# Dense FFN of a fused kernel: fewer plain units, longer segments, sums added into the output by transfers

## The chip, the cores and the metric

One core of a Trainium2 chip runs the whole program. The metric is the device time of one execution in microseconds, measured several times; the profile is one further execution, recorded by the hardware profiler. The engines are PE (matmul), PEld (its weight load), DVE (VectorE), ACT (ScalarE), POOL (GpSimd) and SP (SyncE, which here only issues transfers).

## The reference, cut to what matters

```python
# 1 windowed attention: 4 batches x 8 heads, 576 positions, head size 64, window 64
# 2 soft mixture of experts on x (2304 x 512): 32 slots, 8 experts, w1 512x1024, w2 1024x512
    d = softmax(x @ phi over tokens);  slot_input = d.T @ x
    slot_out[e] = np.maximum(slot_input[e] @ w1[e], 0.0) @ w2[e]
    x = softmax(x @ phi over slots) @ slot_out            # c @ slot_out
# 3 dense FFN on x (2304 tokens x 512), w_in 512x2048, w_out 2048x512, both float64
    h = x @ w_in
    g = np.maximum(h, 0.0) + np.log1p(np.exp(-np.abs(h)))   # softplus
    return (g @ w_out).astype(np.float32)
```

## The kernel before, in words

Parts 1 and 2 of the reference fill the first 124 us. There PE, DVE, ACT and the loads share the work, and the change doesn't touch them until the last product of the experts' second layer (`emit_l2`, L865). What follows is called stage 2 here.

In stage 2 the 2304 tokens are 18 tiles of 128, in five groups of 4, 4, 4, 4 and 2 (`GROUPS`), and the 2048 hidden columns are 16 units of 128. Since the input of the FFN is `c @ slot_out` with 32 slots, `h` is made from `c` (kept transposed as `cT`) and from `slot_out @ w_in` (`wst`, made by the steps WD, WA, WQ, WL, WB, PC, PS from the slots' outputs `soT` and the converted `w_in`), so one matmul gives the 128 hidden columns of a unit for a whole group of tokens.

Both FFN weights come as float64 in `raw` (16 + 16 pieces of 512 KB) and are made float32 on the chip by four operations of 512 columns each (`conv`, step C): a scaling (ACT L970 or DVE L972), and three of integers on DVE (L976, L977, L978).

The first `NN` = 8 units are plain units. For each item (a unit for a group of tiles): H, a matmul 128x512 (L1144); G, softplus on ACT (L1148); GH, its rounding `gh` on ACT (L1009); GL, the rest `gl` = g - gh on DVE (L1012); and for each tile Y, three matmuls 128x512 (L1168 to L1170: gh x high, gh x low, gl x high part of w_out) that add in a PSUM bank. The units of a group go in slabs (`SLABS`, up to two per group). At the end of a group's first slab the bank is copied to `part` in SBUF by ACT (step O, L1009), and at the end of its second slab DVE adds the bank to `part` (L1178).

The other 8 units go in `NP` = 4 pairs, by block products: for two units and a group of tiles, seven products of sums of blocks replace eight. DVE and ACT form the sums on the side of the weights (TA, TB, TC, TK, TM, TH, TL into `thi`, `tlo`) and of the tokens (G2, XA, XB, XC, HG, LG, HX, LX into `shl`); P is one product, for each pair of tiles three matmuls 128x256 (L1249). After a group's four pairs ACT copies each of seven banks (MC, L1257) and DVE adds it into two or one blocks of `part` (M, L1267 and L1273); SP then stores the group's tiles (L1278, 256 KB each).

Every engine runs its own instructions in the order in which they are written. That order comes from `plan()`, which lists the steps with what each needs, and `arrange()`, which goes through them in order of due time with random shifts (`TWEAKS`). Nothing of it is decided on the chip: an engine whose next instruction lacks an input waits, and all behind it wait.

Of the kernel before, what the change touches and what calls it, by code (L numbers as in the profile page):

```python
# [25 lines left out]
NN = 8  # L26
SLABS = ((0, 1, NN), (0, 2, NN), (0, 3, NN), (0, 4, NN), (0, 4, NN))
# [5 lines left out]
NG, NH = 3, 4  # L33
# [3 lines left out]
NCT = 1  # L37
# [10 lines left out]
L2_END, GOAL, SLACK, NEAR = 6.4, 12.0, 0.65, 0.1  # L48
# [16 lines left out]
def arrange(steps, free, ports, tweaks=(), modes=None, slack=SLACK, near=NEAR):  # L65
# [21 lines left out]
    for k in steps:  # L87
        latest[k] += shift[k]
# [65 lines left out]
def plan():  # L154
# [13 lines left out]

    for h in range(2):
        step(("SO", h), dict(D=0.35), rel=L2_END + 0.42 * h - 0.3)  # L170
        step(("ST", h), dict(E=0.43), [("SO", h)])
        step(("SE", h), dict(A=0.26, D=0.33), [("ST", h)])
    for n, r in enumerate(RAWS):
# [16 lines left out]
        elif kind == "wo":  # L190
            if u == 1:
                deps = [("C", "wo", j, x, 3) for x in range(2)] + [(k, j - 1) for k in ("TH", "TL")]
                deps += used_up(max(j - 4, -1)) if 2 * (j - 4) >= NN else []
# [3 lines left out]
                room = [("Y", i, y) for i, x in enumerate(ITEMS) for y in range(x[4], x[5]) if x[1] in (2 * (2 * j - NN - 4), 2 * (2 * j - NN - 4) + 1, 2 * (2 * j - NN - 3), 2 * (2 * j - NN - 3) + 1)] if 2 * j - NN >= 4 else []  # L197
# [22 lines left out]
    for b in range(NCT, 4):  # L220
        step(("CT", b), dict(E=0.48), [("CE", b - 3), ("WD", 0, 1)])
        step(("CE", b), dict(A=0.52, D=0.61), [("CT", b)])
# [9 lines left out]
    for i, (g, f, first, last, ta, tb) in enumerate(ITEMS):  # L232
        n = 128 * (tb - ta)
        b = HBANK[i]
        step(("H", i), dict(E=n * 0.000456), [unit(f)] + weights(START[g] + ta, tb - ta) + ([held[b]] if b in held else []))
# [4 lines left out]
        if i >= NDIRECT:  # L240
            step(("GH", i), dict(A=0.1 + n * 0.00083, D=0.075 + n / 1920), [("G", i)] + [("Y", i - NH, j) for j in range(4)])
        step(("GL", i), dict(P=n * 0.00238, D=0.075 + n / 960), [("GH", i), ("G", i)])
        for j in range(ta, tb):
            deps = [("GH", i), ("GL", i), ("SH", f), ("SL", f), ("Y", i, j - 1)]
            if first:
                deps += [("O", x, j) for x in range(max(0, i - 24), i)] + [("PS", 0)] * (j == 2) + [("CE", x) for x in ((2,), (1,), (), (3,))[j]]
            else:
                deps += [("Y", x, j) for x in range(max(0, i - 2), i) if ITEMS[x][0] == g]
            step(("Y", i, j), dict(E=0.7), deps, goal=goal)
            goal += 0.7  # L250
            if last:
                step(("O", i, j), dict(A=0.49, D=0.61) if f < SLABS[g][1] else dict(D=0.61), [("Y", i, j)])
# [7 lines left out]
    for s, (g, p) in enumerate(PAIRS):  # L260
# [7 lines left out]
        xs = [(k, s - 1 - (s > 1)) for k in ("HX", "LX")] + [("C",) + RAWS[-1] + (3,)] + [(k, NN // 2 + NP - 1) for k in ("TH", "TL") if s > 1]  # L268
# [7 lines left out]
        for i, (b, x, y) in enumerate(PRODUCTS):  # L276
# [42 lines left out]
def block_kernel(ctx: ExitStack, tc: tile.TileContext, qk, v, phi, w1, w2, w_in, w_out, out):  # L319
# [468 lines left out]
    with tc.manual_schedule():  # L788
# [132 lines left out]
        for b in (*range(NCT), 4):  # L921
            do_ct("E", b)
# [428 lines left out]
```

## Time and profile before

| | before |
|---|---|
| median of 3 runs | 351.93 us (351.89 to 352.76) |
| the profiled execution's own time | 351.86 us |
| its span, first to last instruction | 350.2 us |
| granted TensorE clock, mean | 0.998 |
| PE busy | 338.5 us, 97% |
| DVE busy | 286.6 us, 82% |
| ACT busy | 205.7 us, 59% |
| POOL busy | 65.2 us, 19% (all of it before 130 us) |
| read from and written to memory | 64.63 and 4.72 MB |

The span is the time between the first and the last instruction in the trace, and 1.66 us of the profiled execution lie outside it. Busy shares are means over stages that differ; the places that matter here are read from the stages. Start-to-start distance of two instructions of one kind that follow each other without a wait is what one of them costs its engine's queue; the duration of a single instruction is a little longer, since the next one begins before it ends.

### The profile page before, as it was taken

The page shows a single profiled execution, that of the slowest core. Times are in us where ns is not written, and L with a number is a line of the kernel's source. Part 1 is how long each engine was busy: PE and PEld are TensorE (multiplying, and loading weights), DVE is VectorE, ACT ScalarE, POOL GpSimd, SP SyncE. Part 2 cuts the span into 40 slices and gives each one's busy share as a digit, 9 for nine tenths or more (in the row PEclk, how much of TensorE's full clock was granted, in tenths as well). Part 3 has the DMA queues.
Part 4 walks back from the last instruction along what each step waited for, and adds up shares of the span by engine and source line. Part 5 has one row for each costly group of instructions (what it writes and reads, how often), then busy time and mean ns, then how long its engine had stood idle before and what let it go on. Part 6 is the DMA issues. An engine that isn't in the chain of part 4 may idle for free.

```text
span 350.2 us, 8448 instructions
## 1 busy us (share of the span) xinstructions
PE 338.5 (97%) x3298; PEld 273.4 (78%) x3298; DVE 286.6 (82%) x767; ACT 205.7 (59%) x385; POOL 65.2 (19%) x93
## 2 busy tenths in 40 slices
PE   8899998999999999999999999999999999999994
PEld 6788786877434366887788887788999999999994
DVE  5687776875452289999999996988988999999996
ACT  1676565756330069957976465455658568585660
POOL 4997766862040000000000000000000000000000
PEclk9999999999999999999999999999999999999999
DMA  7999999999999984547476300000000030210304
GB/s 283 410 411 403 411 407 409 407 416 393 405 409 417 414 327 161 185 193 242 137 255 210 120 0 3 1 0 2 0 2 0 2 120 2 83 41 0 122 2 181
DMA packets 18184, 69.89 MB, mean 200 GB/s; under 512 B 2016, under 2 KB 2400, under 8 KB 14304
## 3 DMA queue, kind: packets, MB, share of 16 engines
q1 hardware_dynamic: 18000, 69.09, 51.3%
q8 instruction: 26, 0.43, 0.5%
q10 hardware_dynamic: 144, 0.26, 0.2%
q14 instruction: 14, 0.11, 0.1%
HBM read 64.63 MB, written 4.72 MB: 198 GB/s over the span
## 4 chain that ended last, share of the span: by engine, by line
PE 87%; DVE 5%; issue 2%; DMA 1%; ACT 1%; POOL 1%; SPq 0%; DVEq 0%; POOLq 0%; ACTq 0%
PE m_ps L1249 21%; PE y_ps L1168 10%; PE y_ps L1169 10%; PE y_ps L1170 10%; PE x_ps L508 5%; PE pt_ps L490 5%; PE s_ps L463 4%; PE l_ps L815 4%; PE l_ps L865 4%; PE xt_ps L531 2%; PE h_ps L1144 2%; PE h_ps L1186 2%; DVE part L1267 1%; DMA v_three<-v_d 1%; PE lt_ps L541 1%
## 5 line engine op out<-in xcount | busy, mean ns | idle before, releaser
L1249 PE MATMUL m_ps<-thi,shl 128*128 128x256 f32 x504 | 87.7, 283 | 0.0
L1249 PEld LDWEIGHTS m_ps<-thi,shl 128*128 128x128 f32 x504 | 74.8, 190 | 1.4
L1168 PE MATMUL y_ps<-whl,gh 128*128 128x512 f32 x144 | 57.3, 398 | 0.0
L1169 PE MATMUL y_ps<-whl,gh 128*128 128x512 f32 x144 | 57.2, 397 | 0.0
L1170 PE MATMUL y_ps<-whl,gl 128*128 128x512 f32 x144 | 56.8, 395 | 0.0
L1249 PE MATMUL m_ps<-tlo,shl 128*128 128x256 f32 x252 | 53.0, 283 | 0.0
L474 DVE CUSTOM_DVE_ANT_0 sm<-s_ps,cst_sb 128x128 f32<-128x128 f32 x144 | 32.1, 287 | 12.0 <-PE s_ps L463 11.3
L1249 PEld LDWEIGHTS m_ps<-tlo,shl 128*128 128x128 f32 x252 | 40.0, 190 | 0.0
L481 POOL TENSOR_TENSOR sm<-mx,sm 128x512 f32<-128x512 f32 x36 | 36.6, 1039 | 7.2 <-DVE mx L474 6.3
L1168 PEld LDWEIGHTS y_ps<-whl,gh 128*128 128x128 f32 x144 | 27.0, 188 | 9.4 <-issue 1.7
L1148 ACT ACTIVATE g<-h_ps 128x512 f32<-128x512 f32 (+3 forms) x41 | 22.4, 552 | 19.8 <-PE h_ps L1144 19.3
L1206 ACT ACTIVATE g<-h_ps 128x512 f32<-128x512 f32 (+1 forms) x40 | 22.2, 556 | 19.5 <-PE h_ps L1186 19.3
L1170 PEld LDWEIGHTS y_ps<-whl,gl 128*128 128x128 f32 x144 | 27.0, 188 | 7.0 <-DVE gl L1012 0.6
L1169 PEld LDWEIGHTS y_ps<-whl,gh 128*128 128x128 f32 x144 | 27.1, 188 | 5.8
L484 ACT ACTIVATE sm<-sm 128x512 f32<-128x512 f32 x36 | 22.4, 634 | 11.6 <-POOL sm L481 11.4
L428 ACT COPY pt<-pt_ps 128x512 f32<-128x512 f32 x36 | 19.6, 588 | 11.9 <-PE pt_ps L490 11.6
L1009 ACT CAST gh<-g 128x512 fp32r<-128x512 f32 (+2 forms) x40 | 23.0, 581 | 4.6 <-PE y_ps L1169 4.1
L1012 DVE TENSOR_TENSOR gl<-g,gh 128x512 fp32r<-128x512 f32 (+3 forms) x41 | 25.2, 621 | 0.5 <-ACT gh L1009 0.3
L463 PE MATMUL s_ps<-qkb 64*64 64x128 f32 x576 | 20.7, 276 | 1.3 <-issue 1.2
L977 DVE SCALAR_TENSOR_TENSOR cvx<-raw,cvx 128x512 int32<-128x512 int32 x32 | 21.5, 686 | 0.1
L508 PE MATMUL x_ps<-vd,pt 128*64 128x65 f32 x288 | 21.1, 225 | 0.4 <-ACT sm L484 0.4
L508 PEld LDWEIGHTS x_ps<-vd,pt 128*64 128x64 f32 x288 | 18.4, 137 | 3.8 <-issue 2.2
(180 smaller groups left out, 648.2 us busy)
## 6 DMA issues: line engine op xcount, KB each, us to landing
w1t<-w_d SPq DMA_DIRECT2D x15, 1024.0 KB, 10.8
w2t<-w_d SPq DMA_DIRECT2D x13, 1024.0 KB, 10.3
qkb<-qk_d SPq DMA_DIRECT2D x17, 512.0 KB, 10.0
raw<-w_in_d SPq DMA_DIRECT2D x16, 512.0 KB, 4.8
raw<-w_out_d SPq DMA_DIRECT2D x16, 512.0 KB, 5.6
out_d<-part SPq DMA_DIRECT2D x17, 256.0 KB, 2.3
v_three<-v_d SPq DMA_DIRECT2D x10, 260.0 KB, 8.9
vt<-v_d SPq DMA_DIRECT2D x8, 260.0 KB, 9.1
```

Of the source, the lines that this page charges most:

```text
L463: nc.tensor.matmul(s_ps[2 * t + a][64 * par:64 * par + 64, 128 * p:128 * p + 128], qkb[rows, b, 0, p, 64 * par:64 * par + 64], rhs, start= ...
L474: nc.vector.tensor_tensor_reduce(out=sm[:, p], in0=ps[:, 128 * p:128 * p + 128], in1=mask, scale=-0.125, scalar=3.0e38, op0=ALU.add, op1=A ...
L481: nc.gpsimd.tensor_tensor(out=sm_t[i], in0=mb, in1=sm_t[i], op=ALU.subtract)
L484: nc.scalar.activation(out=sm_t[i], in_=sm_t[i], func=AF.Exp)
L508: nc.tensor.matmul(x_ps[64 * par:64 * par + 64, a, 65 * p:65 * p + 65], pt[:, 128 * p + 64 * par:128 * p + 64 * par + 64], vt[:, 65 * h:65 ...
L1009: (nc.scalar.copy if e == "A" else nc.vector.tensor_copy)(dst, src)
L1012: eng[e].tensor_tensor(out=dst, in0=a, in1=b.bitcast(F32), op=ALU.subtract)
L1148: nc.scalar.activation(out=st["g", i], in_=st["h", i], func=AF.Softplus)
L1168: nc.tensor.matmul(y, st["gh", i][:, ts], hi, start=first, stop=False)
L1169: nc.tensor.matmul(y, st["gh", i][:, ts], lo, start=False, stop=False)
L1170: nc.tensor.matmul(y, st["gl", i][:, ts], hi, start=False, stop=last)
L1249: nc.tensor.matmul(ps[:, 256 * j:256 * j + 256], s_tile(s, a)[:, w * x + 128 * j:w * x + 128 * j + 128], t, start=p == 0 and n == 0 and j ...
```

## The change

Units 6 and 7 become a fifth pair (`NN` 8 to 6, `NP` 4 to 5). The plain units no longer go by groups of four tiles but by segments of six tiles (`SEGS`), which hold six banks and leave bank 6 for H; items are three tiles wide (384 columns). Tiles 0 to 5 are done in two segments (units 0 and 1 first, 2 to 5 last), the other twelve in one.

Step O is now always a copy out of PSUM (ACT, or DVE): into a staging slot, from which a transfer issued by GpSimd writes the tile to the output, or, for the second time of tiles 0 to 5, adds it to the output in memory. Only tiles 16 and 17 stay in SBUF (`last_c`). At a group's end the sums of the seven products are made in a buffer of their own (`c_tile`): ACT writes the first two products of a group, each into two blocks (L1309); the others go by copy (L1312) and DVE addition (L1322, L1326) as before. For groups 0 to 3 a transfer of GpSimd adds each half of the group (512 KB) to the output (L1333); the last group is stored by SP as before.

The transition is also rewritten: the last w2 arrives as two halves, its product is 16 matmuls of 128 columns in one bank, split in two parts; the slots' outputs are summed by one DVE copy of 128 columns, one matmul and two copies; two pieces of `cT` are made after that product's first half instead of earlier. `shl` is two fixed sets of tiles. The order tables (`TWEAKS`, a new `SHIFTS`) are other ones; the core of the rest:

```diff
-NN = 8
-SLABS = ((0, 1, NN), (0, 2, NN), (0, 3, NN), (0, 4, NN), (0, 4, NN))
+NN = 6
+SEGS = ((0, 6, 0, 2), (6, 6, 0, NN), (12, 6, 0, NN), (0, 6, 2, NN))
+CUTS = ((0, 1, 3), (0, 3))
...
-HBANK = [4 + i % 3 for i in range(len(ITEMS))]
-PRODUCTS = ((2, 5, 3), (3, 6, 2), (4, 0, 6), (5, 1, 5), (6, 4, 4), (0, 3, 1), (1, 2, 0))
+HBANK = [6, 4, 5] + [6] * (len(ITEMS) - 3)
+PRODUCTS = ((6, 5, 3), (0, 6, 2), (1, 0, 6), (2, 1, 5), (3, 4, 4), (4, 3, 1), (5, 2, 0))
...
-            else:
-                l2_end.extend(bank(x, "l2_end") for x in (2, 7))
-                parts = [(y, 256 * h, 256, True, True) for h, y in enumerate(l2_end)]
...
+            for a in rows:
+                for kk in range(4):
+                    nc.tensor.matmul(
+                        l2_end[0][32 * kk:32 * kk + 32, 0:128], hTz[e // 2][:, e % 2, 4 * r + a, :], w_tiles["w2", j][a][:, 128 * kk:128 * kk + 128],
+                        start=a == 0, stop=a == 3,
                     )
...
+        emit_l2(N2 - 1, (0, 1))
+        do_ct("E", 4)
+        do_ce("A", 4)
...
+        emit_l2(N2 - 1, (2, 3))
+        do_ct("E", 0)
...
-        def do_so(e, h):
-            o = so[:, 256 * h:256 * h + 256]
-            nc.vector.tensor_tensor(out=o, in0=l2_end[h][:, 0:256], in1=o, op=ALU.add)
+        def do_so(e):
+            copy(e, so_end, l2_end[0][:, 0:128])
+
+        def do_st(e):
+            nc.tensor.matmul(so_ps[:, 0:128], so_end, ident, start=False, stop=True, skip_group_check=True)
...
         def do_o(e, i, j):
-            g, f = ITEMS[i][:2]
-            y = y_t.pop((g, j))
-            if f == SLABS[g][1] - 1:
-                copy(e, part[g, j], y)
+            t = TILE_OF[ITEMS[i][0]] + j
+            y = y_t.pop((ITEMS[i][0], j))
+            again = LAST_O[t][0] != (i, j)
+            if t < START[-1]:
+                x = stages[n_st[0] % len(stages)]
+                n_st[0] += 1
+                copy(e, x, y)
+                nc.gpsimd.dma_start(out=rows(t, 1), in_=x.rearrange("p (t c) -> p t c", t=1), **(dict(accum_op=ALU.add) if again else {}))
             else:
-                nc.vector.tensor_tensor(out=part[g, j], in0=y, in1=part[g, j], op=ALU.add)
+                x = last_c[:, 512 * (t - START[-1]):512 * (t - START[-1]) + 512]
...
+            if k in (5, 6):
+                o, m = both(c_tile(g), ps.rearrange("p (t c) -> p t c", t=nj), 0, int(k == 5), 512 * nj)
+                nc.scalar.mul(o, m, -1.0 if k == 5 else 1.0)
+                return
...
+                o = rows(START[g] + nj * a, nj)
+                if g == len(GROUPS) - 1:
+                    nc.sync.dma_start(out=o[:, :, c0:c1], in_=v[:, a, :, c0:c1])
+                else:
+                    nc.gpsimd.dma_start(out=o, in_=v[:, a], accum_op=ALU.add)
```

How the rows stand now, at three places. First DVE from the first conversion on, before (`L1026` adds the last w2's product, `L1012 wst` is a rest of the FFN's first weights):

```order
405 L972 TENSOR_SCALAR cvx<-raw 128x512
406 L976 TENSOR_SCALAR cvx<-cvx 128x512
407 L977 SCALAR_TENSOR_TENSOR cvx<-raw,cvx 128x512
408 L978 SCALAR_TENSOR_TENSOR wit<-raw,cvx 128x512
409 L1026 TENSOR_TENSOR wit<-l_end,wit 128x256 x2
410 L976 TENSOR_SCALAR cvx<-cvx 128x512
411 L972 TENSOR_SCALAR cvx<-raw 128x512
```

And the same place in the changed kernel:

```order
403 L988 TENSOR_SCALAR cvx<-raw 128x512
404 L992 TENSOR_SCALAR cvx<-cvx 128x512
405 L993 SCALAR_TENSOR_TENSOR cvx<-raw,cvx 128x512
406 L994 SCALAR_TENSOR_TENSOR wit<-raw,cvx 128x512
407 L1031 COPY cst_sb<-l_end 128x128
408 L988 TENSOR_SCALAR cvx<-raw 128x512
409 L1031 COPY part<-so_ps 128x256
410 L992 TENSOR_SCALAR cvx<-cvx 128x512
```

The two additions of 256 columns are gone; a copy of 128 columns and one of the two copies to `soT` stand on DVE in their place.

Second DVE late in the plain stage, before (`L1178` is the second O, `tlo` and `txs` sums of a pair's weights):

```order
546 L1178 TENSOR_TENSOR part<-y_ps,part 128x512
547 L1078 TENSOR_TENSOR txs<-wot 128x256
548 L1178 TENSOR_TENSOR part<-y_ps,part 128x512
549 L1012 TENSOR_TENSOR gl<-g,gh 128x512
550 L1178 TENSOR_TENSOR part<-y_ps,part 128x512
551 L1012 TENSOR_TENSOR gl<-g,gh 128x512
552 L1012 TENSOR_TENSOR tlo<-wot,thi 128x512
553 L1012 TENSOR_TENSOR tlo<-txs,thi 128x1280
```

And in the changed kernel, at the part of the plain stage with the second pair's weights:

```order
523 L993 SCALAR_TENSOR_TENSOR cvx<-raw,cvx 128x512
524 L994 SCALAR_TENSOR_TENSOR wot<-raw,cvx 128x512
525 L994 SCALAR_TENSOR_TENSOR wit<-raw,cvx 128x512 x2
526 L992 TENSOR_SCALAR cvx<-cvx 128x512
527 L1034 TENSOR_TENSOR t<-txs,t 128x1280
528 L1034 TENSOR_TENSOR gl<-g,gh 128x384
529 L993 SCALAR_TENSOR_TENSOR cvx<-raw,cvx 128x512
530 L1034 TENSOR_TENSOR gl<-g,gh 128x384
531 L994 SCALAR_TENSOR_TENSOR wot<-raw,cvx 128x512
```

The additions of O have left DVE; conversions stand between the `gl` of the plain units up to the end of that stage.

Third GpSimd's queue after the first stage, in the changed kernel:

```order
64 L920 TENSOR_TENSOR cc_1968<-lnat,cc_1968 128x2x32
65 L1213 DMA out_d<-part 128x512 x6
66 L1152 CAST identr<-cst_sb 128x128
67 L1213 DMA out_d<-part 128x512 x16
68 L1333 DMA out_d<-part 128x2x512 x8
69 L1402 UNCONDITIONAL_BRANCH
```

Before, that queue ended with the one cast; now 22 transfers of a tile and 8 of two tiles are issued there, and the cast stands behind the first six.

## Rows read from the trace of the kernel before

**Rows 1.** Windows: busy us of each engine, its instructions, PE clock, DMA share, GB/s.

```profile
130.00:140.00 10.00, 10.00 (x51) 7.21 (x51) 9.90 (x21) 9.77 (x23) 0.00 (x0) 1.00 0.52 177
140.00:150.00 10.00, 10.00 (x46) 8.13 (x45) 9.90 (x20) 9.92 (x20) 0.00 (x0) 1.00 0.64 215
...
130.70:203.60 72.90, 72.90 (x326) 56.93 (x325) 72.40 (x137) 55.18 (x105) 0.00 (x0) 1.00 0.53 183
...
210.00:220.00 10.00, 10.00 (x48) 7.16 (x47) 6.74 (x12) 5.25 (x8) 0.00 (x0) 1.00 0.01 2
...
260.00:270.00 10.00, 10.00 (x82) 9.82 (x82) 8.54 (x11) 6.81 (x13) 0.00 (x0) 1.00 0.00 0
```

**Rows 2.** Timeline of PE: start, us, line, operation, tiles, how many in a row.

```profile
130.86 0.48 PE L1168 MATMUL y_ps<-whl,gh 128*128 128x512 f32 x1
...
147.82 0.40 PE L1168 MATMUL y_ps<-whl,gh 128*128 128x512 f32 x1
...
148.52 0.40 PE L1168 MATMUL y_ps<-whl,gh 128*128 128x512 f32 x1
...
248.11 0.64 PE L1249 MATMUL m_ps<-thi,shl 128*128 128x256 f32 x4
...
248.83 0.64 PE L1249 MATMUL m_ps<-thi,shl 128*128 128x256 f32 x4
...
344.83 0.28 PE L1249 MATMUL m_ps<-thi,shl 128*128 128x256 f32 x1
```

**Rows 3.** Chain that ended last, one matmul group from it.

```profile
216.76 1.00 PE wq_ps L1111 x8
```

**Rows 4.** Timeline of DVE.

```profile
121.21 0.43 DVE L972 TENSOR_SCALAR cvx<-raw 128x512 f32<-128x512 f32 x1 [4.61 <-DMA raw<-w_in_d]
...
124.67 0.86 DVE L1026 TENSOR_TENSOR wit<-l_end,wit 128x256 f32<-128x256 f32 x2 [1.06 <-PE l_end L865]
...
130.78 0.41 DVE L972 TENSOR_SCALAR cvx<-raw 128x512 f32<-128x512 f32 x1
...
131.65 0.54 DVE L1012 TENSOR_TENSOR gl<-g,gh 128x384 fp32r<-128x384 f32 x1
132.12 0.41 DVE L976 TENSOR_SCALAR cvx<-cvx 128x512 int32<-128x512 int32 x1
...
148.11 0.42 DVE L976 TENSOR_SCALAR cvx<-cvx 128x512 int32<-128x512 int32 x1
148.44 0.69 DVE L978 SCALAR_TENSOR_TENSOR wit<-raw,cvx 128x512 int32<-128x512 int32 x1
149.04 0.69 DVE L1012 TENSOR_TENSOR whl<-wot,whl 128x512 fp32r<-128x512 f32 x1
...
202.22 1.48 DVE L1012 TENSOR_TENSOR tlo<-txs,thi 128x1280 fp32r<-128x1280 f32 x1
203.62 1.89 DVE L1012 TENSOR_TENSOR gl<-g,gh 128x512 fp32r<-128x512 f32 x3
```

**Rows 5.** Groups of DVE, window 130.7 to 203.6: busy us, mean ns, idle before.

```profile
L977 DVE SCALAR_TENSOR_TENSOR cvx<-raw,cvx 128x512 int32<-128x512 int32 x25 | 16.7, 686 | 0.0
L1012 DVE TENSOR_TENSOR gl<-g,gh 128x512 fp32r<-128x512 f32 x20 | 13.6, 686 | 0.0
...
L1178 DVE TENSOR_TENSOR part<-y_ps,part 128x512 f32<-128x512 f32 x4 | 2.8, 688 | 0.2 <-PE y_ps L1170 0.2
```

**Rows 6.** Groups, window 244 to 345.

```profile
L1273 DVE TENSOR_TENSOR part<-part,m 128x1024 f32<-128x1024 f32 x12 | 14.6, 1221 | 1.9 <-ACT m L1257 1.8
```

**Rows 7.** Timeline of the end, all engines.

```profile
345.32 1.60 DVE L1267 TENSOR_TENSOR part<-part,m_ps 128x256 f32<-128x256 f32 x4
345.76 1.67 SPq L1278 DMA_DIRECT2D out_d<-part  x3
```

**Rows 8.** DMA issues of the page: KB each, median us from issue to landing.

```profile
raw<-w_out_d SPq DMA_DIRECT2D x16, 512.0 KB, 5.6
out_d<-part SPq DMA_DIRECT2D x17, 256.0 KB, 2.3
```

More of the change, by code (lines that the diff above doesn't have):

```diff
@@ L36 @@
 NDIRECT = 1
-NCT = 1
 NWC = NWC0 + NWC1 + 2
@@ L196, in plan @@
                 step(("TC", j), dict(D=tt(256)), deps + [("TB", j)])
-                room = [("Y", i, y) for i, x in enumerate(ITEMS) for y in range(x[4], x[5]) if x[1] in (2 * (2 * j - NN - 4), 2 * (2 * j - NN - 4) + 1, 2 * (2 * j - NN - 3), 2 * (2 * j - NN - 3) + 1)] if 2 * j - NN >= 4 else []
+                late = [("Y", i, y) for i, x in enumerate(ITEMS) for y in range(x[4], x[5])]
+                room = [k for k in late if ITEMS[k[1]][1] < 2] if j == 6 else late if j == 7 else []
                 ROOM[j] = room
@@ L218, in plan @@
             step(("PS", n), dict(D=0.33 if w == 1 else 0.61), [("PC", n)])
-    for b in range(NCT, 4):
+    step(("CE", 0), dict(A=0.52, D=0.61), rel=SUMS + 0.3)
+    for b in range(1, 4):
         step(("CT", b), dict(E=0.48), [("CE", b - 3), ("WD", 0, 1)])
@@ L234, in plan @@
         b = HBANK[i]
-        step(("H", i), dict(E=n * 0.000456), [unit(f)] + weights(START[g] + ta, tb - ta) + ([held[b]] if b in held else []))
+        step(("H", i), dict(E=n * 0.000456), [unit(f)] + weights(TILE_OF[g] + ta, tb - ta) + ([held[b]] if b in held else []) + [("H", 0)] * (0 < i < 3))
         held[b] = ("G", i)
@@ L251, in plan @@
             if last:
-                step(("O", i, j), dict(A=0.49, D=0.61) if f < SLABS[g][1] else dict(D=0.61), [("Y", i, j)])
+                t = TILE_OF[g] + j
+                again = LAST_O[t][0] != (i, j)
+                step(("O", i, j), dict(D=0.61) if again and t >= START[-1] else dict(A=0.49, D=0.61), [("Y", i, j)] + [("O", *LAST_O[t][0])] * again)
         goal += n * 0.000456
@@ L854, in block_kernel, with emit_l2 @@
         l2_end = []
-        def emit_l2(j):
+        def emit_l2(j, rows=range(4)):
             e, r = divmod(j, 2)
             if j < N2 - 1:
-                parts = [(l2_ps, 0, 512, j == 0, j == N2 - 2)]
-            else:
-                l2_end.extend(bank(x, "l2_end") for x in (2, 7))
-                parts = [(y, 256 * h, 256, True, True) for h, y in enumerate(l2_end)]
-            for y, o, n, first, last in parts:
                 for a in range(4):
                     nc.tensor.matmul(
-                        y[32 * a:32 * a + 32, 0:n], hTz[e // 2][:, e % 2, 4 * r + a, :], w_tiles["w2", j][a][:, o:o + n],
-                        start=first, stop=last,
+                        l2_ps[32 * a:32 * a + 32, :], hTz[e // 2][:, e % 2, 4 * r + a, :], w_tiles["w2", j][a],
+                        start=j == 0, stop=j == N2 - 2,
+                    )
+                return
+            if not l2_end:
+                l2_end.append(bank(2, "l2_end"))
+            for a in rows:
[3 more added lines that the diff above has]
+                        start=a == 0, stop=a == 3,
                     )
@@ L1047, in do_c, with slot @@
             st["c", kind, j, u][k](e)
+        slots = []
+        def slot(n):
+            while len(slots) <= n:
+                slots.append(wpa.tile([128, 2048], F32R, tag="w", name="whl" if len(slots) < NN // 2 else "t"))
+            return slots[n]
         def do_sh(e, m):
@@ L1064, in t_tiles @@
             if j not in t_hl:
-                t_hl[j] = [wpa.tile([128, 2048], F32R, tag="w", name=n) for n in ("thi", "tlo")]
+                n = 2 * (j - NN // 2)
+                t_hl[j] = [wpx.tile([128, 2048], F32R, tag="w", name="t") if x in (5, 6) else slot(NN // 2 + x - 2 * (x > 6)) for x in (n, n + 1)]
             return t_hl[j]
```

151 lines of the change are left out of this document (85 added, 66 removed).

## The prediction

> **What bounds the kernel now.** I read the windows first [rows 1], to see which engine has no free time in which stage. PE is busy for 10.00 of 10 us in every window from 130 us on, at clock 1.00. So in stage 2 the end is PE's: whatever is taken from PE's queue comes off the time, as long as PE gets its inputs. The reader is to see the second engine too: from 130.7 to 203.6 us DVE is busy for 72.40 of 72.90 us, so it is as full as PE, and only later has it free time (6.74 of 10 us from 210, 8.54 from 260). ACT is at 9.77 and 9.92 of 10 us in the first 20 us and at 55.18 of 72.90 over the stage.
>
> Second, the timeline of PE [rows 2], for what a step costs: three Y matmuls take 0.70 us (147.82 to 148.52), six matmuls of P 0.72 us (248.11 to 248.83), so 0.233 and 0.12 each. The first Y starts at 130.86, the last P matmul at 344.83.
>
> Third, the timeline of DVE [rows 4] by distance of starts: a 512-column L976 0.33 us, L978 0.60, the 1280-column rest of the weights 1.40, a 384-column `gl` 0.47. The groups of its full stretch [rows 5] show nearly no idle time with a named cause.
>
> Fourth, how far DVE runs behind PE. The changed rows matter here, so I added up each queue by those distances, in the order in which its instructions stand. Before, DVE's work up to the end of a `gl` exceeds PE's work up to the matmul that reads it by 7.3 us at most (four places in the first 8 us of the plain stage), then by 1.4 to 6.6 us for 70 us, and after that DVE is ahead. So before, DVE is full because it has work that it may do early, and not because PE waits for it.
>
> **The change, part by part.** *PE.* Two plain units leave: 2 x 18 tiles x 0.70 = 25.2 us. A pair comes: 7 products x 9 pairs of tiles x 3 matmuls = 189 x 0.12 = 22.7 us [rows 2]. H keeps its columns (16 units x 2304), cut into 384 instead of 512, some 0.1 us. By PE's queue alone: -2.4 us.
>
> *DVE in sum.* The 18 additions of O (0.60 each) go: -10.8 us. Eight of the twelve additions L1273 go to ACT; they last 1.22 us [rows 6], about 1.14 from start to start: -9.1. Five scalings and two rests of weights go: -2.9. The fifth pair brings 14 us of sums and rests. Together about -8.7 us. In the pair stage DVE gets air. But in the plain stage it does not: PE's plain stage shrinks from 113.5 to 87.3 us by its queue, while all conversions and the first pair's weights still have to be done in it, and the O additions that left stood mostly behind it (4 in the full stretch [rows 5]).
>
> *Where DVE ends up.* In the new order I take the `gl` that DVE reaches after 60 integer operations of L993 and L994 (60 x 0.60 = 36.1), 36 operations at 0.335 (12.1), 29 `gl` of 384 (13.6), 19 operations of 512 (11.4), two of 1280 (2.8) and 3.2 of small ones: 79.2 us of DVE. PE comes to the matmul that reads it after 260 Y (60.5), 30 H of 384 (30 x 0.175 = 5.2) and 4.4 of the FFN's first weights: 70.1 us. DVE is 9.1 us behind, and it is already 8.4 to 9.0 behind at 6, 12 and 15 us of PE's queue, where before the largest was 7.3. So DVE now sets when PE gets there.
>
> *The start.* Before, DVE works from 121.21 [rows 4], with waits until the w2 product: what it has done by 130.78 is 7.1 us, so its work counts as from 123.68. The change replaces two additions (0.43 each, 124.67) by copies of 128 and 256 columns (0.2 + 0.34 us) and does half of the last product before the last half of w2 lands: I take 0.35 us earlier, 123.35. The first Y hardly moves (it needs the same first conversions), which costs nothing since DVE decides behind it.
>
> *DVE's loss.* From 130.78 to 203.62 the queue sum is 71.3 us [rows 4, 5], the clock says 72.85: 1.5 us lie in small gaps and late starts that no cause is named for. I charge 1.5 us again, because 99% busy [rows 1] leaves little that could be slack; the lower bound is 0. Then the `gl` is ready at 123.35 + 1.5 + 79.2 + 0.1 = 204.15; PE's queue counts as from 204.15 - 70.1 = 134.05. It has 209.7 us up to its last matmul: 343.75, against 344.83 [rows 2], -1.1. Behind this place comes no group of `wq` matmuls (1.00 us each, waits for DVE around them [rows 3]; before, two of four stood late in the plain stage) and no `gl` that is later, so PE isn't delayed a second time.
>
> *ACT.* Its sum grows by some 16 us (24 copies for 18, eight of 1024 columns, bounded by two of 512, the fifth pair), where it has 55.18 of 72.90 busy. But all H behind the third go through one bank: H, softplus, H take turns, and each turn that ACT is late for falls on PE or on the next `gl`. From the full ACT of 130 to 150 us [rows 1] I charge 0.4 us (bounds 0 and 1.5).
>
> *GpSimd's transfers.* No row shows a transfer from GpSimd or one that adds. The nearest are SP's stores: 256 KB land 2.3 us after issue [rows 8]. Nine staging slots and 22 tiles: a slot comes back only after nine further O, at least 9 x 0.70 us of PE, so 6 us or more. Hidden at up to 6 us; I take nothing. The two last additions of 512 KB start when DVE still has 7.8 us of work before its end and 3.3 us pass after that, 11 us in all. SP's rate would need 4 x 2.3 = 9.2 us even one after the other. Nothing, too. *The end* is as before: last DVE additions, three stores of SP [rows 7].
>
> **Sum.** -1.1 + 0.4 = -0.7 us on 351.86, the profiled execution; the median of the runs is 0.07 above that, so 351.3 in round numbers.
>
> **The rivals.** *DVE loses nothing* (28%). If the 1.5 us were room that DVE could afford, since PE didn't wait for it, and ACT keeps its turns: 123.35 + 79.2 + 0.1 - 70.1 = 132.55, last matmul at 342.25, -2.6: 349.3 us. For it: `gl` shows no idle time with a cause. Against: the losses were there at 99% busy.
>
> *GpSimd and DVE hold each other up* (13%): slower. 22 transfers are issued in the stage in which DVE has no air. A 512-column L976 takes 0.33 us where two-input operations of the same width take 0.60 [rows 4], so it runs in another mode; if every second issue had to wait for one, or made one wait, for 0.33 us, DVE would be 11 x 0.33 = 3.7 us later, and PE with it: 355.0 us. It decides from 1.8 us in all, 0.08 us for each issue. Against it: all of GpSimd's work before ended ahead of this stage, so no row speaks. The Trainium skill ("SBUF — State Buffer", "Who interferes with whom" and the trap "DVE blocks DMA" in "two separate sides") says that VectorE's copies, casts and scalar operations in their fast mode lock a port that GpSimd needs to write the descriptors of its transfers, so that one waits for the other's whole instruction; no run here shows it yet. By that rule alone the waiting side could as well be GpSimd, which has nothing else to do, and the price nothing.
>
> *Additions into memory are slow at the end* (6%): the two last transfers decide from 11 us on; at twice SP's time, 18.4 us, the end comes 7 us later, at 358.7. *ACT and the single bank of H set the pace* (6%): some 5 us of turns in the first 20 us; at 0.1 us lost in each of 30 turns +3.0, so 353.9.
>
> **Chances and range.** 47% for the forecast with its own range 350.3 to 352.6 (ACT's and the start's bounds), 28, 13, 6 and 6% for the rivals. 0.3% (1.06 us) is about what a measurement of this kernel can tell. Faster, below 350.9: 27 of the first rival and 11 of the forecast, 38%. Slower, above 353.0: 21 of the rivals' 25 and 2 of the forecast, 23%. Same: 39%. The range 349.0 to 353.6 cuts off some 6% of the first rival and 14% of the others.
>
> **What would show it.** In the profile after, PE's idle time should lie in the first 75 us of the plain stage, before Y's third matmul, released by DVE's `gl`, in total 2 to 3 us, with DVE near 99% busy there; afterwards PE full and DVE with more idle time than before. DVE without its 1.5 us of loss would speak for the first rival. L992 or copies of DVE that last longer than 0.42 us while a transfer is issued would speak for the second; a last transfer that lands behind SP's for the third; H waiting for ACT's softplus for the fourth. I would be wrong at the root if PE's idle time came from elsewhere, say weights that land late because the tiles of `raw` come free later.

## The result

| | before | changed |
|---|---|---|
| median | 352.22 us (351.89 to 352.76, 5 runs) | 354.53 us (353.25 to 355.55, 5 runs) |
| ratio | | 1.0065, interval 1.0047 to 1.0082 |
| profiled execution, its span | 351.86, 350.2 us | 354.53, 352.8 us |
| PE, DVE, ACT, POOL busy | 338.5, 286.6, 205.7, 65.2 us | 340.8, 276.6, 220.1, 89.1 us |

The changed kernel is slower by 0.65%. The forecast was 351.3 us, its range ended at 353.6: it was wrong in sign and in size. (Beside later experiments the same kernel was timed once more: 353.46 us, ratio 1.0038, interval 1.0023 to 1.0053.)

First the windows of the changed kernel, columns as in [rows 1]:

```profile
140.00:150.00 10.00, 9.40 (x41) 6.94 (x40) 9.91 (x21) 9.35 (x21) 4.27 (x7) 1.00 0.94 324
150.00:160.00 10.00, 9.37 (x44) 6.49 (x43) 8.95 (x18) 4.94 (x11) 0.00 (x0) 1.00 0.70 240
...
130.70:203.60 72.90, 71.06 (x326) 53.87 (x324) 70.92 (x137) 58.09 (x119) 8.72 (x15) 1.00 0.67 232
```

PE, which had no free time here before [rows 1], now lacks 1.84 us of 72.90. DVE too lost 1.5 us of busy time, and from 150 to 160 us it is busy for 8.95 only. From 140 to 150 us the DMA engines are at 0.94, and POOL is busy for 4.27 us, where before it did nothing.

Who waits for what, from the waits view: first PEld and PE from 120 us on, then DVE from 126 to 212 (total us, times, longest).

```profile
PEld wq_ps L1141 <- DVE wit L994: 2.1, 3, 1.1
PEld y_ps L1200 <- DVE gl L1034: 2.1, 7, 0.4
...
PEld wp_ps L1154 <- POOL identr L1152: 1.0, 1, 1.0
PEld h_ps L1174 <- ACT g L1178: 1.0, 3, 0.4
```

```profile
PE wq_ps L1141 <- DVE wit L994: 0.9, 2, 0.6
PE wp_ps L1154 <- POOL identr L1152: 0.6, 1, 0.6
```

```profile
DVE cvx L988 <- DMA raw<-w_in_d: 1.0, 1, 1.0
DVE part L1031 <- ACT part L1031: 0.8, 1, 0.8
DVE gl L1034 <- ACT gh L1031: 0.7, 1, 0.7
```

PE's weight loads wait for DVE, as forecast, 2.1 us for `gl` and 2.1 for the converted weights `wit`. But in the view of PE itself only the second shows (0.9 us), beside 0.6 us for a cast of GpSimd: the forecast had the engine right, and `gl` isn't what PE waits for longest. And DVE has three waits with a cause where before it had next to none [rows 5]. Each is followed below to its origin.

**The start.** Timeline of DVE from its first conversion:

```profile
121.17 0.43 DVE L988 TENSOR_SCALAR cvx<-raw 128x512 f32<-128x512 f32 x1 [7.32 <-DMA raw<-w_in_d]
...
122.87 0.69 DVE L994 SCALAR_TENSOR_TENSOR wit<-raw,cvx 128x512 int32<-128x512 int32 x1
125.48 0.29 DVE L1031 COPY cst_sb<-l_end 128x128 f32<-128x128 f32 x1 [1.92 <-PE l_end L886]
...
126.87 0.42 DVE L1031 COPY part<-so_ps 128x256 f32<-128x256 f32 x1 [0.76 <-ACT part L1031]
...
129.44 0.43 DVE L992 TENSOR_SCALAR cvx<-cvx 128x512 int32<-128x512 int32 x1
```

It waits for the last w2 product for 1.92 us (before 1.06, [rows 4]), then 0.76 for ACT. By its queue it has done 4.48 us of work by 129.44 (the distances of the prediction: four operations of 0.60, four of 0.335, a copy of 0.34, two small ones of 0.2), so its work counts as from 124.96. The forecast had 123.35. The timelines of PE and of ACT show why DVE waits for them:

```profile
123.75 1.03 PE L1014 MATMUL so_ps<-cst_sb,wit 128*128 128x32 f32 x8
124.70 0.64 PE L886 MATMUL l_end<-w2t,hTz 128*32 128x128 f32 x16
```

```profile
125.98 0.59 ACT L956 CAST cT<-c_ps 128x512 fp32r<-128x512 f32 x1 [1.66 <-PE c_ps L940]
126.46 0.38 ACT L1031 COPY part<-so_ps 128x256 f32<-128x256 f32 x1
```

The last product's second half stands on PE behind the sum of the slots' outputs. The two copies of `so_ps` are split between ACT and DVE, and ACT's stands behind a copy of `cT`.

**GpSimd's transfers.** Timeline of POOL:

```profile
141.21 2.43 POOL L1213 DMA_DIRECT2D out_d<-part  x4 [36.20 <-ACT part L1031]
145.46 0.55 POOL L1213 DMA_DIRECT2D out_d<-part  x1 [1.81 <-ACT part L1031]
146.93 0.54 POOL L1213 DMA_DIRECT2D out_d<-part  x1 [0.93 <-ACT part L1031]
147.47 0.78 POOL L1152 CAST identr<-cst_sb 128x128 fp32r<-128x128 f32 x1
```

The cast that PE's `wp` needs comes at 147.47, behind six transfers; that is the 1.0 us wait of the weight load above, and 0.6 us of PE. In the same 6 us SP issues two loads (143.10). One piece of the chain that leads to DVE's next work, and DVE itself:

```profile
143.47 7.70 DMA raw<-w_in_d
```

```profile
144.02 0.42 DVE L992 TENSOR_SCALAR cvx<-cvx 128x512 int32<-128x512 int32 x1
144.36 0.68 DVE L994 SCALAR_TENSOR_TENSOR wit<-raw,cvx 128x512 int32<-128x512 int32 x1
...
151.27 0.43 DVE L988 TENSOR_SCALAR cvx<-raw 128x512 f32<-128x512 f32 x1 [0.95 <-DMA raw<-w_in_d]
```

The 512 KB took 7.7 us to land, and DVE waits 0.95 us for them. Its operations during the issues last as long as before (0.42 and 0.68, [rows 4]), and all 32 of L992 lie between 0.41 and 0.45 us (min, median and max in ns):

```profile
L992 DVE TENSOR_SCALAR cvx<-cvx x32: 412/420/446, 121.6 to 215.5; 128x512 int32<-128x512 int32 x32
```

The usual times to landing stand on the page:

```profile
raw<-w_in_d SPq DMA_DIRECT2D x16, 512.0 KB, 5.2
...
out_d<-part POOLq DMA_DIRECT2D x22, 256.0 KB, 4.9
out_d<-part POOLq DMA_DIRECT2D x8, 512.0 KB, 6.2
```

A second lot of transfers is issued from 171 to 177 us. Of two loads issued behind it (177.62 us) ACT waits for one; ACT's scaling is 0.89 us late, its `gh` after it, and DVE's `gl` waits 0.7 us (third row of DVE's waits):

```profile
186.22 0.68 ACT L986 ACTIVATE cvx<-raw 128x512 f32<-128x512 f32 x1 [0.89 <-DMA raw<-w_in_d]
```

**First Y and end.** Timeline of PE, the end of all engines below it:

```profile
132.78 0.48 PE L1198 MATMUL y_ps<-whl,gh 128*128 128x512 f32 x1
...
346.71 1.72 PE L1288 MATMUL m_ps<-t,shl 128*128 128x256 f32 x13
...
348.67 1.32 SPq L1331 DMA_DIRECT2D out_d<-part  x3
```

The first Y is 1.9 us later than before [rows 2]. The last matmul starts at 346.71 + 1.72 - 0.28 = 348.15 us (before 344.83), and SP's stores end the kernel, as before [rows 7].

### The profile page after: what moved, and what is told of

It reads as the page before. It is cut to its first block, busy times and chain, and to the rows that moved or that the text cites. A ratio compares the mean times of both kernels' runs of the same rounds, so it can differ in the third digit from the quotient of the medians.

```text
span 352.8 us, 8779 instructions
## 1 busy us (share of the span) xinstructions
PE 340.8 (97%) x3416; PEld 278.5 (79%) x3416; DVE 276.6 (78%) x757; ACT 220.1 (62%) x410; POOL 89.1 (25%) x123
## 4 chain that ended last, share of the span: by engine, by line
PE 80%; DVE 9%; DMA 4%; issue 3%; ACT 2%; POOL 1%; SPq 0%; DVEq 0%; POOLq 0%; ACTq 0%
PE m_ps L1288 31%; PE x_ps L525 5%; PE s_ps L480 5%; PE pt_ps L507 5%; DMA raw<-w_in_d 4%; PE l_ps L832 4%; PE y_ps L1198 4%; PE y_ps L1199 4%; PE l_ps L877 4%; PE y_ps L1200 4%; PE h_ps L1227 3%; PE xt_ps L548 2%; DVE cvx L993 2%; PE warm_ps L392 2%; PE lt_ps L558 1%
## 5 line engine op out<-in xcount | busy, mean ns | idle before, releaser
L1288 PEld LDWEIGHTS m_ps<-t,shl 128*128 128x128 f32 x945 | 119.0, 190 | 1.8
L1288 PE MATMUL m_ps<-t,shl 128*128 128x256 f32 x945 | 120.4, 283 | 0.0
L1200 PE MATMUL y_ps<-whl,gl 128*128 128x512 f32 x108 | 43.2, 400 | 0.0
L1198 PE MATMUL y_ps<-whl,gh 128*128 128x512 f32 x108 | 43.0, 398 | 0.0
L1199 PE MATMUL y_ps<-whl,gh 128*128 128x512 f32 x108 | 42.8, 396 | 0.0
L1213 POOL DMA_DIRECT2D out_d<-part x22 | 14.4, 669 | 108.4 <-ACT part L1031 108.2
L1333 POOL DMA_DIRECT2D out_d<-part x8 | 9.5, 1370 | 104.8 <-DVE part L1322 65.7
L1200 PEld LDWEIGHTS y_ps<-whl,gl 128*128 128x128 f32 x108 | 20.3, 188 | 6.7 <-DVE gl L1034 2.1
L1198 PEld LDWEIGHTS y_ps<-whl,gh 128*128 128x128 f32 x108 | 20.3, 188 | 6.7 <-issue 1.7
L1034 DVE TENSOR_TENSOR shl<-cvx,shl 128x1280 fp32r<-128x1280 f32 (+1 forms) x13 | 18.0, 1386 | 8.3 <-ACT shl L1031 8.3
L1199 PEld LDWEIGHTS y_ps<-whl,gh 128*128 128x128 f32 x108 | 20.3, 188 | 3.4
L1178 ACT ACTIVATE g<-h_ps 128x384 f32<-128x384 f32 (+2 forms) x37 | 17.8, 482 | 4.3 <-PE h_ps L1174 4.1
L1034 DVE TENSOR_TENSOR gl<-g,gh 128x384 fp32r<-128x384 f32 (+2 forms) x37 | 19.8, 540 | 0.7 <-ACT gh L1031 0.7
```

Of the source, the lines that this page charges most:

```text
L1034: eng[e].tensor_tensor(out=dst, in0=a, in1=b.bitcast(F32), op=ALU.subtract)
L1198: nc.tensor.matmul(y, st["gh", i][:, ts], hi, start=first, stop=False)
L1199: nc.tensor.matmul(y, st["gh", i][:, ts], lo, start=False, stop=False)
L1200: nc.tensor.matmul(y, st["gl", i][:, ts], hi, start=False, stop=last)
L1288: nc.tensor.matmul(ps[:, 256 * j:256 * j + 256], s_tile(s, a)[:, w * x + 128 * j:w * x + 128 * j + 128], t, start=p == 0 and n == 0 and j ...
```

## The experiments

The theories. **A**: DVE sets PE's pace in the plain stage, so what DVE loses at the start and in waits comes through to the end. **C**: GpSimd's transfers cost, by what stands behind them in its queue and by the loads that they meet. Against them stand the other rivals of the prediction: GpSimd and DVE lock each other, ACT and the single bank of H set the pace, the additions are slow at the end. Ratios are against the kernel before on the same chip (its medians there 352.02 to 352.18 us), with 95% intervals. The kernels were timed in five sets (the first two on one chip, each other on a chip of its own) and are best compared within their set.

**First set.** *a*: the second half of the last w2 product ahead of the slots' sum, and both copies of `so_ps` on ACT, ahead of a copy of `cT`.

```diff
+        emit_l2(N2 - 1, (2, 3))
         so_ps = bank(5, "so_ps")
         for kk in range(4):
             nc.tensor.matmul(so_ps[:, 32 * kk:32 * kk + 32], ...)
-        emit_l2(N2 - 1, (2, 3))
...
+        se = [(t, "A", k) for t, e, k in plan_order if k[0] == "SE"]
...
-        for t, e, k in arrange(steps, dict(FREE, E=L2_END - 0.1), PORT, TWEAKS):
+        for t, e, k in rest[:n] + se + rest[n:]:
```

> The changed kernel with one part of its transition put right: the second half of the last w2 product stands ahead of the sum of the slots' outputs, and both copies to soT go to ACT, ahead of the piece of cT that stood before them, so that DVE waits less (1.92 us for the product and 0.76 us for ACT in the changed kernel) and loses one copy. Theory A (DVE sets PE's pace in the plain stage, and what it loses at the start isn't regained): DVE's conversions run 1.0 to 1.6 us earlier from 127 us on, the first P and the last matmul come about 1.2 us earlier, 353.3 us. Theory B (ACT with the single bank of H, or loads, set the pace): the first Y may come earlier, but the end moves by less than 0.3 us.

352.42 us, 1.0010 (0.9992 to 1.0028); the changed kernel itself, in the third set, has 1.0038 with an interval that just overlaps. DVE's timeline:

```profile
124.69 0.29 DVE L1031 COPY cst_sb<-l_end 128x128 f32<-128x128 f32 x1 [1.03 <-PE l_end L886]
...
128.27 0.29 DVE L1034 TENSOR_TENSOR wst<-wp_ps,wst 64x128 fp32r<-64x128 f32 x1 [0.89 <-ACT wst L1031]
```

The wait for the product falls from 1.92 to 1.03, the one for ACT's copy is gone; 0.89 comes back as a wait for ACT's `wst`. By DVE's queue that leaves some 0.5 us of gain (its work counts as from 124.45).

*b*: the first six transfers left out. *c*: all of GpSimd's transfers left out (the condition of b never true, and the call of L1333 removed). The diff of b:

```diff
-                nc.gpsimd.dma_start(out=rows(t, 1), in_=x.rearrange(...
+                if n_st[0] > 6:
+                    nc.gpsimd.dma_start(out=rows(t, 1), in_=x.rearrange(...
```

> The changed kernel without the first six output transfers of GpSimd (tiles 0 to 5 of units 0 and 1 are left out of the output). In the changed kernel they lie at 141 to 147 us beside two loads of raw, of which one lands 7.7 us after its issue and DVE waits 0.95 us for it. Theory C (the transfers slow the loads, and the loads DVE and PE): that load lands in 4 to 5.5 us, DVE's wait at 150 us goes, the end comes 1.0 us earlier, 353.5 us. If the load is late by itself (issued late, since its slot comes free late): no change.

> The changed kernel without any transfer of GpSimd (tiles 0 to 15 aren't written). Theory A: as without the first six, 353.5 us, since the others meet loads that have time. Rival (GpSimd's issues hold up DVE or ACT everywhere): 352 us or less, with shorter DVE and ACT operations.

b 353.26 us, 1.0032 (1.0016 to 1.0048): in its profile the cast is early and the wait for the load at 151 us is gone. c 352.72 us, 1.0008 (0.9991 to 1.0025). The two intervals overlap, and both meet that of the changed kernel (1.0023 to 1.0053), so these two alone don't show what the transfers cost; i and k below do. But even without any transfer the kernel isn't faster than before, so they aren't the whole cause.

*d*: 28 of DVE's 32 operations L992 left out.

```diff
-            st["c", kind, j, u][k](e)
+            if k != 1 or j < 1:
+                st["c", kind, j, u][k](e)
```

> The changed kernel without the second of the four operations of a conversion for 28 of 32 pieces (28 x 0.335 us = 9.4 us less on DVE in the plain stage; the converted weights are wrong). Theory A: PE's waits for gl, for wq and for the FFN's first weights go, PE loses only what it lost before the first Y, and the end comes 3 to 4.5 us earlier, 350.0 to 351.5 us. Theory B (ACT with one bank of H): less than 1 us earlier.

351.21 us, 0.9972 (0.9958 to 0.9986). 28 x 0.335 = 9.4 us off DVE bring the time below that of before. By itself that doesn't yet show that the change made DVE the bound; the control is j.

**Second set.** *e*: the cast issued after the third copy of `cT`, ahead of all transfers. *g*: a and e together. *h*: g and d together.

```diff
-            if n == 2:
-                nc.gpsimd.tensor_copy(identr, selr)
...
+            if k[0] == "CT":
+                n_ct[0] += 1
+                if n_ct[0] == 3:
+                    nc.gpsimd.tensor_copy(identr, selr)
```

> The changed kernel with GpSimd's cast of identr issued ahead of its first six transfers instead of behind them (in the changed kernel it starts at 147.47 us and PE waits 1.0 us for it, of which 0.6 us stop the matmul). If this queueing is what the first six transfers cost: their whole 1.2 us, 353.3 us. If the late load of raw is the larger part: 0.3 to 0.6 us earlier, 354.0 us, with DVE's wait of about 1 us for raw at 150 us still there.

> The corrected transition and the cast first, nothing else. Both theories: 352.4 us of the transition alone less 0.3 to 0.6 us, 351.9 us, that is no change against the kernel before, since DVE still sets the pace in the plain stage.

> The corrected transition, the cast first, and 28 conversions without their second operation (9.4 us less on DVE; the converted weights are wrong): PE's queue is then to be the only limit behind the first Y. Theory A: the first Y at 131.9 us, last matmul 209.7 to 211 us later, 342 to 343, time 348.5 us (from 346.9 with no wait at all to 349.5). If more than 2 us of waits remain, another limit than DVE exists behind the first Y.

e 353.40 us, 1.0028 (1.0010 to 1.0045); g 352.52, 1.0011 (0.9992 to 1.0029); h 350.67, 0.9943 (0.9922 to 0.9965). From e to g the start gives 0.9 us, with intervals that overlap; from g to h DVE's operations give 1.9 us, with intervals that don't. In h the first Y starts at 131.69, and the last matmul at 343.6, 211.9 us later. The expectation had 209.7 to 211 us and a time up to 349.5, and missed: some 2 us above the sum of 209.7 remain that the relief of DVE doesn't remove. PE's waits name 0.3 us of them (for ACT's `g`); the rest is open, and the sum itself may be too small. That 343.6 is near the forecast's 343.75 is chance, since the forecast had DVE hold PE back by more than it does here.

*f*: g, and also GpSimd instead of DVE for the rest of `whl` of four units, with the six transfers held back behind the first of these.

```diff
-            sub(e, l, wt.pop(("wo", j, u)), h)
+            sub("P" if m > 1 else e, l, wt.pop(("wo", j, u)), h)
+            if m == 2:
+                for x in held_back:
+                    nc.gpsimd.dma_start(**x)
```

> The corrected transition, the cast first, the low halves of units 2 to 5 (4 x 0.60 us) subtracted on GpSimd instead of DVE, and the first six transfers issued behind the first of these, at about 153 us. Theory A with C: the loads of raw land in 4 to 5.5 us again, DVE ends the plain stage 2.4 us + 1 us earlier than with the transition alone, 350.3 us, faster than before. Rival (GpSimd's subtractions take about 1.04 us each and Y waits for them, or hold DVE up): 352 us or more.

358.75 us, 1.0183 (1.0153 to 1.0214), a miss. Timelines of GpSimd, and of DVE beside it:

```profile
147.44 1.65 POOL L1034 TENSOR_TENSOR whl<-wot,whl 128x512 fp32r<-128x512 f32 x1 [16.76 <-ACT whl L1031]
149.02 3.46 POOL L1092 DMA_DIRECT2D out_d<-part  x6
152.50 2.74 POOL L1034 TENSOR_TENSOR whl<-wot,whl 128x512 fp32r<-128x512 f32 x2
```

```profile
147.24 0.68 DVE L994 SCALAR_TENSOR_TENSOR wot<-raw,cvx 128x512 int32<-128x512 int32 x1
147.84 1.79 DVE L994 SCALAR_TENSOR_TENSOR wit<-raw,cvx 128x512 int32<-128x512 int32 x1
...
150.59 1.52 DVE L1034 TENSOR_TENSOR gl<-g,gh 128x384 fp32r<-128x384 f32 x1
152.04 2.06 DVE L988 TENSOR_SCALAR cvx<-raw 128x512 f32<-128x512 f32 x1
```

DVE's operations stretch from 0.68 to 1.79, from 0.55 to 1.52 and from 0.43 to 2.06 us around GpSimd's subtractions and the six transfers behind the first. The mutual hold-up of the second rival exists on this chip, but in the changed kernel itself, where GpSimd only issues beside DVE, the rows above don't show it. One of the three lengthened operations of f, the `gl` from 150.59 to 152.11, does lie within the six issues, before GpSimd computes again; why it took 1.52 us is open. The Trainium skill ("SBUF — State Buffer", "Who interferes with whom") says that the port pair that the two engines share is locked by one at a time. For GpSimd's computing the trace agrees in kind (1.79 and 2.06 us above).

**Third set.** *j*: the control, the kernel before without the same 28 operations (L976 there; the diff is that of d). *i*: g, and two further operations of conversions ahead of the first `wst`, to fill DVE's wait of 0.89 us. *k*: i without any of GpSimd's transfers. *l*: the changed kernel again.

```diff
+        early = [("C", "wo", 0, 1, 0), ("C", "wi", 0, 1, 1)]
...
+        n = next(n for n, x in enumerate(plan_order) if x[2] == ("PS", 0))
+        for t, e, k in plan_order[:n] + moved + plan_order[n:]:
```

> The kernel before, with the second operation of 28 conversions left out (9.4 us less on DVE; the converted weights are wrong): the same relief that made the changed kernel 3.3 us faster. Theory A (before, DVE was full but not what PE waits for): within 0.4 us of the kernel before, 352.0 us. If DVE paced PE there too: 1 us or more faster.

> The corrected transition, the cast first, and on DVE the rest of the first weights (wst, 64x128), which waits 0.8 to 0.9 us for ACT at 128 us, behind two conversion operations that stood behind it. Theory A: DVE's count starts 0.8 us earlier, and the end comes 0.8 us earlier than with the two corrections alone, 351.7 us. If DVE waits for something else in its place at the start: no change, 352.5 us.

> The kernel with the three corrections without any transfer of GpSimd (tiles 0 to 15 aren't written). Theory C: the waits for raw that are left (ACT waits 0.8 us for a load at 182 us and DVE 0.7 us for ACT at 184) go, 0.7 us earlier than with the three corrections, 351.0 us. If the transfers cost only what they did to the cast: the same time as with the three corrections.

> The changed kernel itself once more, on the chip of these runs: 354.5 us, 0.65% slower than the kernel before.

j 352.05 us, 1.0000 (0.9987 to 1.0014): the same relief gives the kernel before nothing. Windows of j, then of h:

```profile
130.70:203.60 72.90, 72.82 (x327) 57.34 (x328) 66.48 (x114) 54.92 (x106) 0.00 (x0) 1.00 0.54 186
```

```profile
130.70:203.60 72.90, 72.53 (x336) 56.30 (x337) 66.93 (x116) 60.74 (x123) 8.89 (x16) 1.00 0.67 237
```

In both DVE now has 6 us of air. Before, PE was full anyway (72.90) and stays so; in the changed kernel PE was at 71.06 and rises to 72.53. That is theory A.

i 352.78 us, 1.0018 (0.9998 to 1.0039): DVE's wait for `wst` is gone from its profile, and yet there is no gain on g (0.8 us was expected). k 351.38 us, 0.9976 (0.9960 to 0.9993). From i to k the transfers alone are 1.4 us, with intervals that don't meet; that is theory C, with twice the size that was expected for k (0.7 us). The cast stands ahead of the transfers in both, so none of it is the cast's. The two loads that SP issues at 143.10 in the changed kernel, and at 142.00 in k, show how (from the DMA view, 140 to 152 us, the changed kernel first):

```profile
raw<-w_in_d SPq DMA_DIRECT2D x2, 512.0 KB, 6.6
```

```profile
raw<-w_in_d SPq DMA_DIRECT2D x2, 512.0 KB, 4.4
```

In the nine profiles with the six transfers bunched beside these two loads (the changed kernel, a, d, e, g, h, i, l, o) their median is 5.2 to 6.9 us from issue to landing, in b, c and k 4.1 to 4.5. In b they are issued at 143.09, as early as in the changed kernel, so it isn't a late issue.

l 353.46 us, 1.0038: in its profile DVE's wait for the load at 151 us and that for `gh` at 187 us are missing, the wait for the product is 2.34. So the waits for loads come in some executions of the changed kernel and not in others.

**Fourth set.** *m*: i, with the plain stage's transfers held back and issued one behind each `gl`, paced by a GpSimd copy of one column. *n*: m with three scalings moved from DVE to ACT (the last two lines).

```diff
+            if held_back:
+                nc.gpsimd.tensor_copy(tiny[:, 0:1], st["g", i][:, 0:1])
+                nc.gpsimd.dma_start(**held_back.pop(0))
...
+            if k[0] == "C" and k[4] == 0 and k[2] in (3, 4):
+                e = "A"
```

> The kernel with the three corrections, and GpSimd's transfers of the plain stage issued one for each item (about every 2.3 us, behind a copy of one column that GpSimd takes from that item) instead of three to six together; its kernel without transfers was 1.4 us faster. Theory C (bursts of transfers meet the loads of raw): most of that comes back, no wait of DVE for raw at 150 us, 351.6 us, ratio 0.998. If the sum of the transfers' bytes is what costs, or GpSimd's own work: no change, 352.8 us, ratio 1.002.

> The same with three scalings of 512 columns that stood on DVE behind 149 us (3 x 0.335 us) moved to ACT, which has free time there. Theory A (DVE paces PE up to 205 us): 0.8 to 1.0 us earlier than with the spacing alone, 350.7 us. If ACT paces: the same or later.

m 354.83 us, 1.0090 (1.0060 to 1.0119); n 352.59, 1.0012 (0.9996 to 1.0028). m says nothing about spacing, since its pacing copy got stuck. Timeline of POOL, and the wait that follows from it:

```profile
137.90 8.30 POOL L1190 COPY tiny<-g 128x1 f32<-128x1 f32 x1 [7.95 <-ACT g L1176]
...
169.54 8.66 POOL L1190 COPY tiny<-g 128x1 f32<-128x1 f32 x1 [16.71 <-ACT g L1176]
```

```profile
ACT g L1176 <- POOL tiny L1190: 4.6, 3, 2.4
```

These two copies of one column last 8.30 and 8.66 us, a third 6.61, the median of the 16 0.50; ACT can't reuse `g` meanwhile. Others beside the same DVE took 0.20 to 0.67, so what holds up three of them is open. n is 2.2 us faster than m, where 0.8 to 1.0 was expected; in its profile ACT waits 0.7 us for such copies instead of 4.6, so this isn't the worth of the scalings either.

**Fifth set.** *p*: as m, with the pacing by a copy of one column on ACT, inside the staging slot. *o*: i with n's three scalings on ACT. *q*: p with them.

```diff
-                nc.gpsimd.tensor_copy(tiny[:, 0:1], st["g", i][:, 0:1])
-                nc.gpsimd.dma_start(**held_back.pop(0))
+                x, args = held_back.pop(0)
+                nc.scalar.copy(x[:, 0:1], x[:, 0:1])
+                nc.gpsimd.dma_start(**args)
```

> The kernel with the three corrections, and the plain stage's transfers issued one for each item, each held back by a copy of one column that ACT makes inside its own staging slot (GpSimd computes nothing, unlike in m_spaced, where its one-column copies took up to 8.7 us and ACT waited for them). Theory C (bursts meet the loads of raw): up to 1 us earlier than with the corrections, ratio 0.999. If the bytes cost and not the bursts: 1.002 or, by ACT's 16 extra copies, a little later.

> The kernel with the three corrections and three scalings of 512 columns moved from DVE to ACT behind 149 us, nothing spaced. Theory A (each microsecond taken from DVE in the plain stage comes off the end): 3 x 0.335 us, 0.8 to 1.0 us earlier than with the three corrections, ratio 0.999. If ACT paces there: the same or later.

> Both together. If both theories hold: 1.5 us earlier than with the three corrections, ratio 0.998, which would be faster than the kernel before by 0.7 us.

p 352.00 us, 0.9996 (0.9986 to 1.0007); o 353.23, 1.0028 (1.0012 to 1.0044); q 352.10, 0.9992 (0.9982 to 1.0003). o and q differ in when the transfers are issued, and in ACT's copies of one column that q has more: q is 1.1 us faster, with intervals that don't meet. In p and q the two loads land 4.2 and 4.1 us after issue, as without transfers. Timelines of POOL and DVE in p:

```profile
143.18 0.76 POOL L1192 DMA_DIRECT2D out_d<-part  x1 [13.30 <-ACT part L1191]
145.67 0.58 POOL L1192 DMA_DIRECT2D out_d<-part  x1 [1.73 <-ACT part L1191]
```

```profile
149.18 0.42 DVE L988 TENSOR_SCALAR cvx<-raw 128x512 f32<-128x512 f32 x1
```

One transfer each 2.5 us at first instead of four within 2.4, and the conversion that waited until 151.27 starts at 149.18 without a wait. Moving scalings to ACT gains nothing: in o DVE waits for ACT's scalings instead,

```profile
DVE cvx L992 <- ACT cvx L986: 2.2, 3, 1.5
```

and q ties with p. p and q do all of the changed kernel's work and tie with the kernel before; no version that does all of the work beat it by more than can be measured.

## Why the prediction was wrong

The frame held: DVE paces PE in the plain stage (d and h against j). The `gl` of the prediction's place and the matmul that reads it can be found in the profile after:

```profile
207.21 0.55 DVE L1034 TENSOR_TENSOR gl<-g,gh 128x384 fp32r<-128x384 f32 x1
```

```profile
207.81 0.50 PE L1200 MATMUL y_ps<-whl,gl 128*128 128x512 f32 x1
```

The `gl` is ready at 207.76, and the matmul starts at 207.81. Less the 79.2 us of work that the prediction counts, DVE's work counts by then as from 128.5: 124.96 and its later losses. Less its 70.1 us, PE's queue counts as from 137.7. The forecast was 134.05. So the rule from DVE's queue to PE's was right and its entries were not:

| step, as the prediction put it | forecast | the profile after | later by, us |
|---|---|---|---|
| start: "0.35 us earlier" | 123.35 | 124.96 | 1.6 |
| transfers: "I take nothing", a load that lands late at 151 | 0 | 1.04 | 1.0 |
| transfers, a load that makes ACT and `gl` late near 186 | 0 | 0.75 | 0.75 |
| "I charge 1.5 us again" | 1.5 | 1.8, what is left of the 128.5 | 0.3 |
| "PE isn't delayed a second time" | 0 | 137.7 becomes 138.45 | 0.7 |
| ACT and the bank of H: "I charge 0.4 us" | 0.4 | within the rows above | -0.4 |
| the end "as before", last matmul to end of span | 5.37 | 4.65 | -0.7 |

Together some 3.3 us (352.8 of span and 1.73 around it, against 351.2). The rows are read from one execution; their causes stand as follows.

*The start* failed first. That the change "does half of the last product before the last half of w2 lands" was taken as a gain for DVE. But that product's second half stands on PE behind the slots' sum, and the sum's copies are split over two engines, each behind other work: a hand-over PE, DVE, PE, ACT and DVE in 2 us, of which the prediction priced the copies and not the waits. Up to the first `wst`, counted from its first conversion, DVE loses 3.8 us in the changed kernel, 3.2 in a, 2.7 in i and 2.4 before. So the orders of a and i take back 1.1 us of it. In the time this isn't shown as clearly: from e to g it is 0.9 us, with intervals that overlap, and i gains nothing on g.

*GpSimd's transfers* failed second, and here the step looked in the wrong place. It asked when a staging slot comes free and when the last addition lands; both were right (nothing waits for either). It did not ask what stands behind the transfers on GpSimd (the cast, which the order rows showed) nor what other transfers are under way in the same microseconds. Taking the transfers away (i to k) is worth 1.4 us, spreading them (o to q) 1.1, both without the cast, which is ahead of the transfers in these four: what is shown is the cost of the loads that land late. The cast's own share isn't settled: e and l differ by 0.06 us, on two chips. With l's profile free of both waits the rows 1.0 and 0.75 of the table belong to the one execution and not to every one.

*A second delay of PE* (0.7 us): the prediction took it as nothing because no `wq` group stands behind the place, and none does (the last starts at 203.97). PE's own view lists no wait there. Its weight loads wait 0.5 us for two later `gl` and 0.4 us for ACT's `g`; that these make up the 0.7 us isn't shown.

The rivals: the second had the sign (355.0), not the mechanism, since DVE's operations don't lengthen during the issues; that its number is near the result is luck. *DVE loses nothing* is refuted by its waits. The additions at the end cost nothing: the last one lands at 350.49 us, and SP's last store, which ends the kernel, at 351.86. ACT and the single bank of H show as 1.0 us of the weight loads' waits in the waits view, far from the 3.0 that it takes; ACT matters in the way that it is late for DVE (o). The last sign of the prediction, weights that land late, came with 0.95 us at 151, though not for its reason: the load was issued in time.

## What to carry to other kernels

When two engines are full in one stage, add up each one's queue from the hand-over at the stage's start, waits included. Work taken off the engine that sets the pace came off the time here (from 1.0011 to 0.9943, g to h), and the same relief where that engine is only full was worth nothing (1.0000, j). A transfer that nobody waits for still costs if it is issued in a burst while a load that somebody does wait for is under way; space such transfers, and look at what stands behind them on the issuing engine. Small work given to GpSimd beside a full DVE cost more than it took off here (f, m); measure it before relying on it.

## What the runs showed of the hardware

- Three of 16 copies of one column on GpSimd lasted 8.30, 8.66 and 6.61 us, the median 0.50 (m). Issuing transfers of 256 KB took it 2.43 us for four in a row, then 0.55 and 0.54 (141.21 to 147.47 us in the changed kernel), and lengthened no operation of DVE.
- Beside GpSimd's subtractions, DVE's 0.68 us operation took 1.79, and a scaling of 0.43 us took 2.06 (f).
- Two loads of 512 KB landed 5.2 to 6.9 us after issue beside six transfers of GpSimd in 6 us (median of the two, nine profiles), and 4.1 to 4.5 without these or with them spread (b, c, k, p, q).
- Adding transfers of 512 KB land 6.2 us after issue, 256 KB from GpSimd 4.9 (SP's 256 KB before: 2.3, [rows 8]).
